# Ten transposed K blocks instead of six kept between two passes over a KV cache

## The chip, the cores and the metric

The kernel runs on one core of one Trainium2 chip. The metric is the device time of one execution in microseconds (us). A core has a matrix engine (TensorE, PE in the profile; PEld is its weight load), a vector engine (VectorE, DVE), a scalar engine (ScalarE, ACT), GpSimd (POOL), a queue engine that here only issues loads (SyncE, SP), and 16 DMA engines between the off-chip memory (HBM) and the on-chip memory of 128 partitions (SBUF). PE writes its results to PSUM, from which DVE or ACT copy them ("evacuation").

## The reference

Two kinds of layers alternate twice on one token `x` of 1024 elements: attention over a cache, then an MLP with squared ReLU. Both attention layers use the same weights and the same cache, and so do both MLPs. The reference returns the output and the gradients of everything for a given `grad_out`.

```python
x = x + A(layernorm(x));  x = x + B(layernorm(x))
x = x + A(layernorm(x));  x = x + B(layernorm(x))

# A: 32 query heads on 4 key/value heads, 65536 cached positions, head size 128
q = (x @ wq)                      # 1024 -> 32 x 128
scores = q . k_cache * 128**-0.5  # 8 query heads share one key/value head
o = softmax(scores) . v_cache
return o @ wo
# B: 3584 hidden
h = x @ w1 + b1;  r = max(h, 0);  return (r * r) @ w2 + b2
```

K and V are 64 MiB each in bfloat16 (4 groups of 16 MiB); their gradients, which are written, have the same size.

## The kernel before, in words

**Four passes over the cache.** Pass 1 is the forward of the first attention layer (L1), then comes the first MLP (L2), pass 2 is the forward of the second attention layer (L3), then the second MLP and its backward (L4); passes 3 and 4 are the backward of the two attention layers. Each pass reads all of K and V. The "first boundary" is the MLP L2 between pass 1 and pass 2. Pass 1 takes the groups in order 0, 1, 2, 3 (`ORD1`), pass 2 in order 3, 2, 1, 0 (`ORD2`), so that the group that ends pass 1 begins pass 2.

**Items and blocks.** A group has 512 chunks of 128 positions. An *item* is 8 chunks (64 items a group, `IPG`), a *block* is 4 items, 1 MiB of K or V (16 blocks a group). `attn_fwd` runs a software pipeline over 256 items (`pipeline`): at step i it does `kT` of item i, `kS` of item i-2 and `v8` of item i-78 (`TLEAD` = 2, `LAGV` = 78).
- `kT` transposes 8 K chunks on PE into a PSUM tile `ps_tr` (L656) and evacuates them to one of five blocks of `small`, on DVE or ACT (`evac`, L152 and L155, whichever has the smaller planned load).
- `kS` multiplies them with the queries (L675); every 64 chunks ACT copies the scores to a score buffer (L680) and DVE takes maxima (L681). Behind a group's last item, `stats` forms the maximum and ACT the exponentials (L704) into `eT`.
- `v8` multiplies 8 V chunks with the exponentials (L718).
Since V of a group needs the group's maximum, V runs 78 items behind K.

**Side work.** `bg` holds functions that run at a given step. `q_rest` loads 8 rows of `wq` (768 KB each) and multiplies them with the token, for the queries of the three later groups: row k at step 20 + 4k. `out_group` loads the two slabs of `wo` of a finished group and multiplies (products on L399, in `mv_slab`).

**The memory areas.** SBUF holds 14 areas of 8 KB per partition (`area[0]` to `area[13]`, two to a `pair`), the exponentials `eT1` and `eT3` of both layers, and `small`. `pair[10]` (areas 10, 11) and `pair[12]` (areas 12, 13) are the score buffers `S0` and `S1`, used by the groups in turn. Areas 0 to 9 form the ring (`Ring`): each load takes the area that was taken longest ago (`slot`), or, for a wide load of two blocks (2 MiB), a pair whose halves are both in the ring (`wide`). During pass 1 the space of `eT3`, which the second layer fills only later, lends four areas (`e3_halves`); they leave the ring 9 steps before the last group.

**The order of the loads.** All loads of this part are issued by SyncE in one queue, in the order in which they are written; a load waits in it until the readers of its area's former content are done, and what is written behind it waits too. A load has no other place in time: it goes as early as its area and the queue let it. The framework's scheduler may move instructions on an engine; "built order" means the order in which they stand in the finished program.

**What is kept.** In pass 1 the transposed blocks of group 3 that `keep` names stay where `kT` evacuates them. In pass 2 `kT` neither loads nor transposes the blocks in `have`; `kS` reads them where they lie. `kept1` has six: one in the space of each of the four groups of `eT3`, two in `S0`, which the last group of pass 1 does not use (it writes to `S1`).

**Around the boundary.** Behind pass 1 stand `out_group` of group 3, 8 slabs of `B_w1` (L399), 7 slabs of `B_w2`, which are multiplied (L399) and also row-multiplied with `grad_out` for a later gradient (`RowDots`: L421, L422, L457, L468 to L476), then two slabs of `wq` for the first group of pass 2 (`q_first`), all through the ring.

Of the kernel before, what the change touches and what calls it, by code (L numbers as in the profile page):

```python
# [18 lines left out]
def kernel(  # L19
# [27 lines left out]
    G = A_k_cache.shape[1]  # L47
# [20 lines left out]
    IPG = C // 8  # L68
# [48 lines left out]
    def ps_bg(shape, dtype=F32):  # L117
        return ps_small("bg", shape, dtype)
# [50 lines left out]
    area, pair, wides = [], {}, []  # L169
# [5 lines left out]
    e3_halves = [e3_all[:, i * SLOT:(i + 1) * SLOT] for i in range(4)]  # L175
# [4 lines left out]
    def e_area(k, g):  # L180
        return e_tiles[k][g][:, 0:SLOT]

    def part(ap, i, n):
        return ap[:, i * n:(i + 1) * n]
# [11 lines left out]
    class Ring:  # L196
# [35 lines left out]
        def wide(self):  # L232

            best = None
            for w, lo, hi in wides:
                h = [s for a in (lo, hi) for s in self.slots if s["ap"] is a and not s["held"]]
                if len(h) == 2:
                    t = max(s["used"] for s in h)
                    if best is None or t < best[0]:
                        best = (t, w, h)  # L240
            for s in best[2]:
                s["used"] = self.clock
                self.clock += 1
            return best[1], [s["ap"] for s in best[2]]

        def hold(self):

            s = self.last
            s["held"] = True

            def give():
                s["held"] = False
            return give

    ring = Ring()
# [14 lines left out]
    def slab(src, a, n):  # L270
        v = ring.slot()[:, 0:a * n].rearrange("p (a n) -> p a n", n=n)
        nc.sync.dma_start(out=v, in_=src)
        return v
# [109 lines left out]
    def w_rows(W, r0, nk, c0, ncol):  # L383

        return W[r0:r0 + nk * P, c0:c0 + ncol].rearrange("(k p) n -> p k n", p=P)

    def slabs(W, r0, KC, c0, ncol):

        per = max(1, min(KC, SLOT // ncol))
        for k0 in range(0, KC, per):  # L390
            kn = min(per, KC - k0)
            v = slab(w_rows(W, r0 + k0 * P, kn, c0, ncol), kn, ncol)
            for kk in range(kn):
                yield k0 + kk, v[:, kk, :]

    def mv_slab(out, view, kc, KC, ncol, xcol):
        nb_ = ncol // P
        for nb in range(nb_):
            nc.tensor.matmul(out[:, nb:nb + 1], lhsT=view[:, nb * P:(nb + 1) * P], rhs=xcol,  # L399
                             start=(kc == 0 and nb == 0), stop=(kc == KC - 1 and nb == nb_ - 1), skip_group_check=True)  # L400
# [186 lines left out]
    def at(bg, i, fn):  # L587
        bg.setdefault(i, []).append(fn)

    def q_first(L, g):  # L590

        pq = ps_bg([P, R])
        for kc, view in slabs(A_wq, 0, DC, g * GD, GD):
            mv_slab(pq, view, kc, DC, GD, L["nb"][:, kc:kc + 1])
        set_q(L, pq, 0, [g])

    def set_q(L, pq, at_, gs):
        for i, g in enumerate(gs):
            nc.vector.tensor_copy(out=L["qT"][:, g * R:(g + 1) * R], in_=pq[:, (at_ + i) * R:(at_ + i + 1) * R])
            nc.vector.tensor_copy(out=L["qpad"][:, g, :, :], in_=L["qT"][:, g * R:(g + 1) * R].unsqueeze(1).to_broadcast([P, 8, R]))  # L600

    def q_rest(L, gs, bg, i0, step):
        gs = sorted(gs)
        c0, ncol = gs[0] * GD, len(gs) * GD
        assert gs == list(range(gs[0], gs[0] + len(gs)))
        box = {}

        def one(kc):
            if kc == 0:
                box["p"] = ps_bg([P, len(gs) * R])  # L610
            v = slab(w_rows(A_wq, kc * P, 1, c0, ncol), 1, ncol)
            mv_slab(box["p"], v[:, 0, :], kc, DC, ncol, L["nb"][:, kc:kc + 1])
            if kc == DC - 1:
                set_q(L, box["p"], 0, gs)
        for kc in range(DC):
            at(bg, i0 + kc * step, lambda kc=kc: one(kc))
# [8 lines left out]
    def new_layer(x, lname):  # L625
        n, nb, rstd = ln_fwd(x, lname)
        L = dict(n=n, nb=nb, rstd=rstd)
        for key, w, dt in (("qT", HQ, F32), ("oT", HQ, F32), ("oTb", HQ, BF), ("rZ", HQ, F32), ("xo", DC, F32)):
            L[key] = vec.tile([P, w], dt, name=lname + "_" + key)
        L["qpad"] = vec.tile([P, G, 8, R], BF, name=lname + "_qpad")  # L630
        nc.vector.tensor_copy(out=L["xo"][:], in_=x[:])
        return L

    def attn_fwd(L, order, eT, s_areas, more=None, keep=(), have=()):

        kit = items_of(order)
        n = len(kit)
        bg = {}
        if more is not None:
            more(bg, n - 1 + TLEAD)  # L640
        q_rest(L, order[1:], bg, 20, 4)
        for j, g in enumerate(order[:-1]):
            at(bg, LAGV + IPG * (j + 1) + 4, lambda g=g: out_group(L, g))
        kstream, vstream = Stream(Kv, True), Stream(Vv, True)
        state = {}

        def kT(idx):
            g, c8 = kit[idx]
            b, j = divmod(c8, J)
            if g == order[0] and b < len(have):  # L650
                state[("kt", idx)] = blocks(have[b], j // 8)
                return
            kb8 = kstream.items(g, c8)
            pt = ps_tr()
            for i in range(8):
                nc.tensor.transpose(pt[:, i, :], kb8[:, i, :], ident_b[:, :])  # L656
            kt = blocks(keep[b], j // 8) if g == order[-1] and b < len(keep) else KT.next()
            evac(kt[:, :, :], pt[:, :, :])
            state[("kt", idx)] = kt
# [475 lines left out]
    eT1, eT3 = Exps(1), Exps(3)  # L1135
    U, X1 = area[0:5], area[5:10]
    S0, S1 = pair[10], pair[12]
# [3 lines left out]
    L1 = new_layer(x0, "L1")  # L1141
    ORD1, ORD2, ORD3, ORD4 = [0, 1, 2, 3], [3, 2, 1, 0], [0, 1, 2, 3], [3, 2, 1, 0]
# [2 lines left out]
    b2c = col_from_dram(B_b2, D, "b2c")  # L1145
    gx = col_from_dram(grad_out.rearrange("a b d -> (a b d)"), D, "gx")

    kept1 = [e_area(3, g) for g in range(G)] + [area[10], area[11]]
    ring.add(*e3_halves)

    def ahead_of_last(bg, ik):
        at(bg, IPG * (G - 1) - 9, lambda: ring.remove(*e3_halves))
    attn_fwd(L1, ORD1, eT1, [S0, S1], more=ahead_of_last, keep=kept1)


    out_group(L1, ORD1[-1])
# [11 lines left out]
    dg4 = rd4.result()  # L1168
    L3 = new_layer(L2["xo"], "L3")
    q_first(L3, ORD2[0])  # L1170


    VKEEP = 4
# [2 lines left out]
    def fetch_w1(a=None):  # L1176
        v = (a if a is not None else ring.slot())
        w1_slots.append(v)
        nc.sync.dma_start(out=v[:, 0:F], in_=B_w1[len(w1s) * P:(len(w1s) + 1) * P, :])
        w1s.append(v[:, 0:F])  # L1180
# [10 lines left out]
    def wo_block(k, out=None, scalar=True):  # L1191

        v = kept[k][1] if out is None else out
        transpose(kept[k][1], v, scalar)
        woT[k] = [part(v, i, P) for i in range(DC)]

    def ahead_of_end(bg, ik):
        e = ik + 1 - TLEAD + LAGV
        at(bg, e - 28, fetch_wo)
        for k, i in ((0, 4), (1, 7)):  # L1200
            at(bg, e - 12 + 4 * k, lambda k=k, i=i: wo_block(k, part(small, i, 1024), k == 0))
        at(bg, e - 6, lambda: (fetch_w1(area[12]), fetch_w1(area[13])))
    v_areas = attn_fwd(L3, ORD2, eT3, [S1, S0], more=ahead_of_end, have=kept1)
    v_kept = [v_areas[(ORD2[-1], b)] for b in range(NB - VKEEP, NB)]


# [24 lines left out]
    bg = {}  # L1231
# [125 lines left out]
    bg = {}  # L1357
# [67 lines left out]
```

## Time and profile before

| | us |
|---|---|
| median of 3 runs | 2000.78 (1998.74 to 2001.92) |
| profiled execution, its time | 2006.47 |
| profiled execution, its span | 2004.7 |
| pass 1 | 0 to about 368 |
| products of `B_w1` and `B_w2`, layer norm | about 372 to 421 |
| first score product of pass 2 | 423.1 |
| pass 2 until its last V product | 423 to 770 |
| bytes moved by DMA | 798 MB, mean 398 GB/s |
| PE / DVE / ACT busy | 80% / 55% / 51% of the span |

Times inside an execution are in microseconds from the start of the span. A row of groups of instructions gives line, engine, operation, output and input tiles, shape and count. "PEclk" is the granted share of TensorE's full clock. "DMA share" is the mean busy share of the 16 DMA engines (overlap can bring it slightly above 1). On SyncE's timeline a row stands for one or more loads issued, and its duration is that of issuing, not of the transfer.

### The profile page before, as it was taken

The page shows a single profiled execution, that of the slowest core. Times are in us where ns is not written, and L with a number is a line of the kernel's source. Part 1 is how long each engine was busy: PE and PEld are TensorE (multiplying, and loading weights), DVE is VectorE, ACT ScalarE, POOL GpSimd, SP SyncE. Part 2 cuts the span into 40 slices and gives each one's busy share as a digit, 9 for nine tenths or more (in the row PEclk, how much of TensorE's full clock was granted, in tenths as well). Part 3 has the DMA queues.
Part 4 walks back from the last instruction along what each step waited for, and adds up shares of the span by engine and source line. Part 5 has one row for each costly group of instructions (what it writes and reads, how often), then busy time and mean ns, then how long its engine had stood idle before and what let it go on. Part 6 is the DMA issues. An engine that isn't in the chain of part 4 may idle for free.

```text
span 2004.7 us, 66048 instructions
## 1 busy us (share of the span) xinstructions
PE 1599.8 (80%) x30052; PEld 1320.6 (66%) x30052; DVE 1108.3 (55%) x1826; ACT 1032.3 (51%) x1290; POOL 203.3 (10%) x362
## 2 busy tenths in 40 slices
PE   7888776678888867887878876877888878778896
PEld 6888776578787756876777774555555545545463
DVE  4544431255444313745454446876677767787675
ACT  3543432125433313445454436876677667767775
POOL 0000000000000000000000001222122222212221
PEclk9999997679999976998989987999889988899898
DMA  9999999999999996999999996999999999999997
GB/s 395 426 424 421 419 422 413 395 368 376 424 421 419 423 414 272 399 418 409 411 413 393 403 372 261 389 425 424 389 413 407 423 423 383 422 358 422 423 422 293
DMA packets 117316, 798.08 MB, mean 398 GB/s; under 512 B 11548, under 2 KB 11562, under 8 KB 55082
## 3 DMA queue, kind: packets, MB, share of 16 engines
q1 hardware_dynamic: 80986, 608.22, 74.0%
q0 software_dynamic: 29136, 173.04, 20.9%
q10 hardware_dynamic: 6912, 12.59, 1.7%
q8 instruction: 235, 3.85, 0.7%
q14 instruction: 47, 0.39, 0.0%
HBM read 628.11 MB, written 165.69 MB: 396 GB/s over the span
## 4 chain that ended last, share of the span: by engine, by line
PE 39%; DMA 30%; DVE 12%; ACT 11%; issue 7%; POOL 0%; SPq 0%; DVEq 0%; ACTq 0%; POOLq 0%
DMA pair<-in_A_v_cache_dram 13%; DMA out_dram<-pair 8%; PE ps_tr L656 7%; DMA pair<-in_A_k_cache_dram 5%; PE ps_sc L675 4%; ACT small L152 4%; PE ps_tr L909 4%; PE ps_acc L718 3%; PE ps_gg L1071 3%; PE ps_tr L1004 3%; ACT pair L152 3%; DVE pair L155 3%; DVE small L155 2%; PE ps_sc L930 2%; PE ps_gg L1122 2%
## 5 line engine op out<-in xcount | busy, mean ns | idle before, releaser
L155 DVE COPY small<-ps_tr 128x1024 bf16<-128x1024 bf16 x655 | 445.2, 688 | 356.1 <-PE ps_tr L656 197.8
L152 ACT COPY small<-ps_tr 128x1024 bf16<-128x1024 bf16 x385 | 386.6, 1014 | 410.1 <-PE ps_tr L656 234.1
L152 ACT CAST pair<-ps_gg 128x1024 bf16<-128x1024 f32 (+2 forms) x331 | 320.2, 983 | 143.2 <-PE ps_gg L1071 81.8
L155 DVE CAST pair<-ps_gg 128x1024 bf16<-128x1024 f32 x245 | 289.2, 1181 | 115.6 <-PE ps_gg L1071 89.0
L656 PE MATMUL ps_tr<-ident_b,pair 128*128 128x128 bf16 x3456 | 263.4, 225 | 34.6 <-DMA pair<-in_A_k_cache_dram 25.4
L1071 PE MATMUL ps_gg<-pair,small 64*128 64x512 bf16 x1024 | 202.9, 405 | 53.8 <-ACT pair L152 21.5
L656 PEld LDWEIGHTS <-pair 128*128 128x128 bf16 x3456 | 209.5, 101 | 39.7 <-DMA pair<-in_A_k_cache_dram 27.8
L675 PE MATMUL ps_sc<-L_qpad,small 128*128 128x64 bf16 (+7 forms) x3712 | 187.5, 194 | 27.1 <-ACT small L152 13.9
L718 PE MATMUL ps_acc<-eT,pair 128*128 128x64 bf16 x3840 | 167.1, 205 | 44.9 <-DMA pair<-in_A_v_cache_dram 39.6
L718 PEld LDWEIGHTS <-pair 128*128 128x128 bf16 x3840 | 151.9, 104 | 48.5 <-DMA pair<-in_A_v_cache_dram 42.4
L675 PEld LDWEIGHTS <-small 128*128 128x128 bf16 x3712 | 151.5, 99 | 38.5 <-ACT small L152 20.1
L1004 PE MATMUL ps_tr<-ident_b,pair 128*128 128x128 bf16 x1792 | 163.3, 229 | 14.1 <-DMA pair<-in_A_v_cache_dram 12.0
L422 ACT ACTIVATE pair<-pair 128x1024 bf16<-128x1024 bf16 (+1 forms) x125 | 142.1, 1137 | 45.6 <-DVE pair L421 43.6
L909 PE MATMUL ps_tr<-ident_b,pair 128*128 128x128 bf16 x2048 | 153.5, 227 | 10.4 <-DMA pair<-in_A_v_cache_dram 5.4
L1004 PEld LDWEIGHTS <-pair 128*128 128x128 bf16 x1792 | 115.6, 102 | 60.5 <-issue 41.5
L909 PEld LDWEIGHTS <-pair 128*128 128x128 bf16 x2048 | 126.7, 102 | 30.8 <-issue 20.7
L1071 PEld LDWEIGHTS <-small 64*128 64x128 bf16 x1024 | 60.5, 94 | 111.3 <-issue 83.8
L930 PE MATMUL ps_sc<-B_dOpad,small 128*128 128x64 bf16 (+7 forms) x2048 | 103.0, 194 | 21.5 <-DVE small L155 13.9
L1024 PE MATMUL ps_sc<-DOB,small 128*128 128x64 bf16 (+3 forms) x2048 | 111.7, 194 | 0.1
L1024 PEld LDWEIGHTS <-small 128*128 128x128 bf16 x2048 | 86.6, 99 | 36.8 <-issue 32.2
L930 PEld LDWEIGHTS <-small 128*128 128x128 bf16 x2048 | 81.2, 99 | 32.8 <-DVE small L155 17.5
L681 DVE TENSOR_REDUCE pm_all<-pair 128x8 f32<-128x512 f32 x64 | 44.0, 688 | 106.1 <-ACT pair L680 106.1
(262 smaller groups left out, 1966.2 us busy)
## 6 DMA issues: line engine op xcount, KB each, us to landing
pair<-in_A_v_cache_dram SPq DMA_DIRECT2D x70, 2048.0 KB, 19.9
pair<-in_A_k_cache_dram SPq DMA_DIRECT2D x65, 2048.0 KB, 19.5
out_dram<-pair POOLq DMA_DIRECT2D x128, 1024.0 KB, 16.2
pair<-in_A_k_cache_dram SPq DMA_DIRECT2D x97, 1024.0 KB, 12.4
pair<-in_A_v_cache_dram SPq DMA_DIRECT2D x96, 1024.0 KB, 12.8
pair<-in_A_wo_dram SPq DMA_DIRECT2D x24, 1024.0 KB, 20.3
out_dram<-eT POOLq DMA_DIRECT2D x44, 512.0 KB, 15.6
pair<-in_B_w_dram SPq DMA_DIRECT2D x24, 896.0 KB, 16.7
```

Source lines behind the costliest of these rows:

```text
L152: nc.scalar.copy(out=out, in_=in_)
L155: nc.vector.tensor_copy(out=out, in_=in_)
L422: nc.scalar.activation(out=view, in_=view, func=ACTF.Copy, accum_out=ycol)
L656: nc.tensor.transpose(pt[:, i, :], kb8[:, i, :], ident_b[:, :])
L675: nc.tensor.matmul(ps_s[:, slot:slot + w, :].rearrange("p a b -> p (a b)"), lhsT=kt[:, i, :], rhs=L["qpad"][:, g, 0:w, :].rearrange("p a b ...
L681: nc.vector.tensor_reduce(out=pm_all[:, :, c0 // UB], in_=S_sb[:, :, c0:c0 + un], axis=AX.X, op=ALU.max)
L718: nc.tensor.matmul(ps_o[:, :, :].rearrange("p a b -> p (a b)"), lhsT=vb8[:, i, :], rhs=eT[g][:, :, c:c + 8], start=(c == 0), stop=(c == C ...
L909: nc.tensor.transpose(pt[:, i, :], vb8[:, i, :], ident_b[:, :])
L930: nc.tensor.matmul(ps_dp[:, slot:slot + w, :].rearrange("p a b -> p (a b)"), lhsT=vt[:, i, :], rhs=dOpad[:, g, 0:w, :].rearrange("p a b -> ...
L1004: nc.tensor.transpose(pt[:, i, :], vb8[:, i, :], ident_b[:, :])
L1024: nc.tensor.matmul(ps_dp[:, slot:slot + w, :].rearrange("p a b -> p (a b)"), lhsT=vt[:, i, :], rhs=DOB[:, g, 0:w, :].rearrange("p a b -> p ...
L1071: nc.tensor.matmul(pg[:, t2 * 512:(t2 + 1) * 512], lhsT=xt[64 * t2:64 * t2 + 64, blk0 + half, :], rhs=GG[64 * t2:64 * t2 + 64, :, :, :].re ...
```

## The change

- `kept1` becomes ten areas: the four `e3_halves`, areas 10 and 11, and two pairs of the ring. These two pairs are taken out of the ring while the last group of pass 1 runs (`take_pair`, 14 and 22 steps into it), always the pair that was used longest ago. From then on the ring has six areas.
- From 6 steps into the last group to 8 steps behind its K items, `narrow` makes K and V come in loads of one block instead of two.
- `S1` (areas 12, 13) joins the ring behind the last group's exponentials, through the rest of pass 1, the MLP and `q_first`, and then leaves it.
- In pass 2 each kept area outside `S0` joins the ring one step after its last item's scores; the four `e3_halves` leave it at step 52, before the exponentials are written there.
- In pass 2 the rows of `q_rest` come at step 2 + 3k instead of 20 + 4k.

```diff
+        def take_pair(self):
+            halves = self.wide()[1]
+            self.remove(*halves)
+            return halves
...
-    def attn_fwd(L, order, eT, s_areas, more=None, keep=(), have=()):
+    def attn_fwd(L, order, eT, s_areas, more=None, keep=(), have=(), q_at=(20, 4), narrow=None):
...
-        q_rest(L, order[1:], bg, 20, 4)
+        q_rest(L, order[1:], bg, *q_at)
...
+        def width(wide):
+            kstream.wide = vstream.wide = wide
+        for i, wide in zip(narrow or (), (False, True)):
+            at(bg, i, lambda wide=wide: width(wide))
...
-    kept1 = [e_area(3, g) for g in range(G)] + [area[10], area[11]]
+    kept1 = e3_halves + [area[10], area[11]]
     ring.add(*e3_halves)
+    last = IPG * (G - 1)
     def ahead_of_last(bg, ik):
-        at(bg, IPG * (G - 1) - 9, lambda: ring.remove(*e3_halves))
-    attn_fwd(L1, ORD1, eT1, [S0, S1], more=ahead_of_last, keep=kept1)
+        at(bg, last - 9, lambda: ring.remove(*e3_halves))
+        for i in (last + 14, last + 22):
+            at(bg, i, lambda: kept1.extend(ring.take_pair()))
+        at(bg, last + IPG + 7, lambda: ring.add(area[12], area[13]))
+    attn_fwd(L1, ORD1, eT1, [S0, S1], more=ahead_of_last, keep=kept1, narrow=(last + 6, last + IPG + 8))
...
     q_first(L3, ORD2[0])
+    ring.remove(area[12], area[13])
...
     def ahead_of_end(bg, ik):
+        for b, a in enumerate(kept1):
+            if not any(a is x for x in (area[10], area[11])):
+                at(bg, 4 * b + 5, lambda a=a: ring.add(a))
+        at(bg, IPG - 12, lambda: ring.remove(*e3_halves))
...
-    v_areas = attn_fwd(L3, ORD2, eT3, [S1, S0], more=ahead_of_end, have=kept1)
+    v_areas = attn_fwd(L3, ORD2, eT3, [S1, S0], more=ahead_of_end, have=kept1, q_at=(2, 3))
```

## The prediction

> **What bounds the kernel now.** I read the page first (engines, DMA row, chain), then stretches of time, then SyncE's queue around the first boundary, then PE there. The page's DMA row stands at 9 in almost all of its 40 slices, and among the chain's costliest rows are loads. The stretches (columns: span in us; busy us and instructions of PE, PEld, DVE, ACT, POOL; granted clock; DMA share; GB/s) say where this is strict:
>
> ```profile
> PE 39%; DMA 30%; DVE 12%; ACT 11%; issue 7%; POOL 0%; SPq 0%; DVEq 0%; ACTq 0%; POOLq 0%
> ...
> 0.00:320.00 320.00, 263.13 (x6028) 250.23 (x6029) 141.40 (x261) 133.02 (x180) 1.03 (x10) 0.98 1.00 417
> 320.00:380.00 60.00, 35.44 (x786) 33.73 (x782) 2.90 (x17) 6.55 (x17) 0.00 (x0) 0.67 1.00 407
> 380.00:424.00 44.00, 28.78 (x630) 27.46 (x631) 21.21 (x57) 17.30 (x27) 0.00 (x0) 0.50 1.02 392
> 424.00:462.00 38.00, 32.95 (x815) 31.72 (x813) 20.05 (x36) 7.02 (x10) 0.61 (x4) 0.93 0.80 306
> 462.00:766.00 304.00, 238.32 (x5477) 228.19 (x5474) 113.86 (x190) 113.30 (x165) 0.00 (x0) 0.92 1.01 420
> 1060.00:1080.00 20.00, 17.68 (x424) 16.31 (x421) 8.14 (x11) 8.06 (x9) 0.00 (x0) 1.00 1.02 418
> ```
>
> Pass 1 (to about 368) and pass 2 from 462 on are DMA-bound: share 1.00 and 1.01, PE busy for 0.8 of the time. There a load that is left out shortens the pass by its own transfer, whatever PE does. The exception is 424 to 462, the start of pass 2: share 0.80, so 7.6 us of DMA time are lost. SyncE's queue shows why (start, us of issuing, what):
>
> ```profile
> 402.75 0.48 SPq L295 DMA_DIRECT2D pair<-in_A_k_cache_dram  x1
> 403.33 1.78 SPq L272 DMA_DIRECT2D pair<-in_A_wq_dram  x2
> 414.72 0.33 SPq L295 DMA_DIRECT2D pair<-in_A_k_cache_dram  x1
> 417.37 4.55 SPq L272 DMA_DIRECT2D pair<-in_A_wq_dram  x2
> 429.61 0.33 SPq L295 DMA_DIRECT2D pair<-in_A_k_cache_dram  x1
> ...
> 446.34 12.08 SPq L295 DMA_DIRECT2D pair<-in_A_k_cache_dram  x3
> 465.57 0.33 SPq L295 DMA_DIRECT2D pair<-in_A_v_cache_dram  x1
> ...
> SPq L295 <- PE ps_bg L399: 11.2, 2, 7.6
> SPq L295 <- PE ps_tr L656: 10.9, 1, 10.9
> SPq L272 <- PE ps_tr L656: 10.7, 3, 4.2
> ```
>
> The loads wait for PE to leave a ring area (the last three rows: who waited, total us, times, longest). The three K loads from 446.34 are issued at 446.34, 457.62 and 458.04 in the records; from the second on DMA is full again. PE at the same place:
>
> ```profile
> 423.11 5.17 PE L675 MATMUL ps_sc<-L_qpad,eT 128*128 128x64 bf16 x128 [0.49 <-DVE L_qpad L600]
> 428.83 0.74 PE L399 MATMUL ps_bg<-L_nb,pair 128*128 128x1 bf16 x24
> 429.44 1.28 PE L675 MATMUL ps_sc<-L_qpad,pair 128*128 128x64 bf16 x40
> ```
>
> A kept item (8 score matmuls) costs 0.31 us up to 429.4 and 0.23 after; one row of `wq` (24 products) 0.6. A K item that must be transposed costs 0.86 to 1.1 us here, evacuation waits included (40 of them end at 477.3, from 430.7; the last 23 took 19.9 us).
>
> **The change, part by part.** The sum is made on the profiled execution (span 2004.7, time 2006.47, 5.7 over the median of 2000.78) and moved to the median unchanged.
>
> 1. *Four K blocks less to load.* In the built program K reads fall from 250 to 246 MiB. 4.19 MB at the 420 GB/s of 462:766 are 10.0 us. With them go 16 items' transposes (0.45 us of PE each) and their evacuations, which lie beside the DMA and pay nothing directly.
>
> 2. *The start of pass 2* decides whether the 10.0 us arrive. All eight `wq` rows now stand ahead of the first K load in SyncE's queue, and in the built order of PE their products come after 5, 12, 19, 26, 33, 39, 40 and 40 kept items. Slots: rows 0 to 4 go where parts of `B_w2` lay (the last two leave at 414.7 and 417.4), row 5 where the first `wq` slab lay (421.6), row 6 where row 0 lay, row 7 into a consumed kept block. They land by about 430, none is late. The first K pair (blocks 10 and 11) takes the area of rows 2 and 3. PE gets through row 3 at: 16 items and two rows by 429.4, then 9.4 items x 0.23 + 1.2 = 432.8. A load on an empty queue shows its first packet 1.0 us after issue (429.61 to 430.6, 457.62 to 458.6), and 2.1 MB take 5.0: landing 438.8. PE is through its 40 items at 438.4, so it waits for almost nothing. Blocks 12 to 15 and group 2's first pair follow without a gap (areas free by 431, 437.1 and 437.9): 443.8, 448.8, 453.8. Before, group 2's first pair was issued at 457.62 and landed at 458.6 + 5.0 = 463.6. From this load on both kernels send the same loads, so the pass is **9.8 us** ahead. DMA idles more than before up to 434 and less after it. For the queue to stay full PE must leave the pair of block 15 by 468: 438.4 + 24 items x 0.86 to 1.0 = 459 to 462. Bounds: if blocks 10 and 11 wait for the 40th item (438.4), 4.2; if their area is free with row 2 (430.6), 12.0.
>
> 3. *Narrow loads at the end of pass 1.* In the built order 30 loads of 1 MiB stand in place of 15 of 2 MiB. In the packet records a 16 KB packet takes 619 ns and an 8 KB one 317 to 321 (pass 3), so 1 MiB over 16 engines takes 2.48 or 2.54 to 2.57 us: 30 x 0.06 to 0.09 = 1.8 to 2.7, taken as **+2.3**. The bytes are the same, so no gain is possible: low end 0. High end: pass 3 from 1040 to 1120, with the same two narrow streams, five or six areas left and more side work, moves 395 GB/s on average (395, 418, 393, 373); 31.5 MB at 395 instead of 420 is +4.7. I take the packets, since the side work of pass 3 is absent here.
>
> 4. *Six areas in place of ten for items 214 to 263.* A 1 MiB area is wanted again 8 to 9 items before its data is needed, which at 0.5 MiB an item leaves four loads, about 10 us, in the queue; PE needs 3.9 us for the 4 items that one K and one V block feed (32 transposes 1.8, 32 score matmuls 0.9, 32 products 1.1 at full clock), DMA 5.1. Cost 0; the cover is that queue. The products of the second group's `A_wo` (64, 1.9 us) stand whole behind both of its slabs, with four loads in flight, 10 us: 0.
>
> 5. *The score buffer in the ring.* The second V pair of the last group now waits for ACT's exponentials, and every later load queues behind it on SyncE. Before, the last K pair landed at 308.6, PE was through it at 314, the exponentials ran from 319.25 to 324.8. In the narrow order (one block, 4 items, 2.7 us) they end 2.7 + 5.3 + 5.6 = 13.6 us after the last K block. Queued behind that block are four V blocks, one V pair and two `A_wo` slabs, 8.4 MB or 20 us. Hidden, with 6 us to spare; beyond that it would cost one for one.
>
> 6. *Eight areas through the MLP.* Each part of `B_w2` waits for the slab of `B_w1` eight loads earlier, which itself is paced by landing (the products of the last two slabs start at 385.19 and 387.4). Queue never empty: 0. The stretch 390 to 417 is computation and not touched. Dropping areas 12 and 13 from the ring, and adding the kept areas to it, issue nothing.
>
> Sum: -9.8 + 2.3 = **-7.5 us**: 1993.3 on the median. Behind pass 2 the built order is the same but for about a hundred PE instructions and three exchanges of loads, so the lead is carried to the end.
>
> **Rivals.**
>
> *Narrow loads starve the DMA (slower).* If every second narrow load meets an empty queue and pays its 1.0 us lead-in, 15 us go: 2000.8 - 9.8 + 2.3 + 15 = 2008.3. It decides from 0.25 us per narrow load (7.5/30). For it: only six areas, and two streams locked to each other. Against: 1060:1080, share 1.02 at 418 GB/s with as few areas. Chance 0.12. The Trainium skill ("DMA: Bandwidth & Descriptors", Measured) gives 341 GB/s for a lone DMA of 1 MB and 425 for 16 MB, and asks for large batches; by its figure the 31.5 MB would cost an estimated 17 us more and the change would lose some 7. The 418 GB/s of that stretch disagree, because other loads are in flight there.
>
> *The start of pass 2 gives it back (no change).* The first K load is held until the 40th kept item and pass 3's 395 GB/s hold in the tail: -4.2 + 4.7, about 2001.3; with only one of the two, 1996 to 1999. For it: loads before 462 wait for PE already (11.2 us under `ps_bg`), and DMA will idle some 10 us between 410 and 434. Against: PE runs kept items at 0.23 to 0.31 us, so areas come free sooner than now. Chance 0.16.
>
> *That fewer loads are not made* is excluded by the built program's 246 MiB.
>
> **How the numbers follow.** What a measurement of this kernel can tell from no change is 0.2%, 4 us (the three runs shown spread 0.16%). The forecast, a gain over 4 us: 0.72; within 4 us: 0.16; slower: 0.12. The range takes parts 2 and 3 at their ends: -12.0 + 0 gives 1988.8, -4.2 + 4.7 gives 2001.3; it leaves out the starved tail.
>
> **What would show it.** Part 1: K bytes less by 4.19 MB, pass 2 still at 420 GB/s. Part 2: the first K load of pass 2 near 433 (plus the tail's shift), the full queue from about 434 on instead of 458. Part 3: last V landing of pass 1 2 to 3 us later, share 1.00 throughout. Part 5: no gap of the DMA 15 to 20 us after the last K block of pass 1. Wrong it would be if the stretch 250 to 320 showed a share clearly under 1, or if PE in pass 2 waited for K loads beyond the first.

## The result, and the profile after

The changed kernel is faster: 1995.0 us median (1993.3 to 1998.2) against 2001.6 for the kernel before on the same chip, a ratio of 0.997 with a 95% interval of 0.996 to 0.998. That is 6.6 us less, where 7.5 were predicted. Measured again on another chip it gave 1993.3 against 1999.9, 0.9967 (0.9955 to 0.9979).

The stretches of the changed kernel (columns as before: span in us; busy us and instructions of PE, PEld, DVE, ACT, POOL; granted clock; DMA share; GB/s):

```profile
0.00:320.00 320.00, 265.79 (x6024) 250.25 (x6025) 141.02 (x261) 134.36 (x184) 1.04 (x10) 0.97 1.00 414
320.00:380.00 60.00, 35.38 (x762) 33.38 (x758) 2.86 (x17) 5.07 (x12) 0.00 (x0) 0.64 1.00 410
380.00:424.00 44.00, 28.63 (x639) 27.29 (x640) 20.83 (x55) 17.35 (x27) 0.00 (x0) 0.50 0.94 355
424.00:462.00 38.00, 34.15 (x871) 33.66 (x869) 19.50 (x36) 6.13 (x9) 0.61 (x4) 0.85 0.87 348
462.00:766.00 304.00, 237.39 (x5446) 227.75 (x5445) 109.67 (x191) 108.26 (x159) 0.00 (x0) 0.92 1.01 419
```

The DMA-bound stretches are DMA-bound still: 1.00 in pass 1, 1.01 at 419 GB/s from 462 on. At the boundary the idle time of the DMA has moved: less of it after 424 (share 0.87, was 0.80), more before (0.94 in 380 to 424, was 1.02). SyncE's queue there:

```profile
396.43 31.39 SPq L278 DMA_DIRECT2D pair<-in_A_wq_dram  x9
427.87 0.42 SPq L278 DMA_DIRECT2D eT<-in_A_wq_dram  x1
435.02 0.33 SPq L301 DMA_DIRECT2D pair<-in_A_k_cache_dram  x1
435.40 0.42 SPq L301 DMA_DIRECT2D eT<-in_A_k_cache_dram  x1
439.55 4.30 SPq L301 DMA_DIRECT2D pair<-in_A_k_cache_dram  x3
451.07 0.33 SPq L301 DMA_DIRECT2D pair<-in_A_v_cache_dram  x1
```

All ten loads of `wq` stand ahead of the first K load, which is issued at 435.0. The three from 439.55 are issued at 439.55, 443.05 and 443.43 in the records; the one at 443.05 is group 2's first pair, 14.6 us earlier than before (457.62). In the records of landings that pair is complete at 458.4, and at 459.0 in a second execution (e12), instead of 466.9: 8.5 and 7.9 us ahead. PE there:

```profile
438.78 0.74 PE L405 MATMUL ps_bg<-L_nb,pair 128*128 128x1 bf16 x24
439.38 0.27 PE L686 MATMUL ps_sc<-L_qpad,pair 128*128 128x40 bf16 x5
439.51 0.54 PE L405 MATMUL ps_bg<-L_nb,pair 128*128 128x1 bf16 x16
442.67 0.35 PE L405 MATMUL ps_bg<-L_nb,pair 128*128 128x1 bf16 x8 [2.62 <-issue]
442.88 0.78 PE L405 MATMUL ps_bg<-L_nb,eT 128*128 128x1 bf16 x24
443.52 2.72 PE L667 MATMUL ps_tr<-ident_b,pair 128*128 128x128 bf16 x24
```

The 40 kept items are through at 439.5 (predicted 438.4), but the transposes begin at 443.5: a row of `wq` stops in its middle for 2.6 us ("issue": nothing that the profile shows was waited for).

What that was worth shows in the last division of each pass. The line that forms the outputs of a group, first of the kernel before, then of the changed one (last column: first and last start):

```profile
L722 DVE TENSOR_TENSOR L_oT<-ps_acc,L_rZ x8: 166/167/168, 157.6 to 769.7; 128x8 f32<-128x8 f32 x8
```

```profile
L733 DVE TENSOR_TENSOR L_oT<-ps_acc,L_rZ x8: 166/167/168, 157.6 to 762.5; 128x8 f32<-128x8 f32 x8
```

The end of pass 2 is 7.2 us earlier (7.8 in the second execution). The end of pass 1 (fourth of the eight) is at 369.1 instead of 368.1.

**A ledger of bytes.** The packet records give, for each kernel, the time at which it has moved as many bytes as the kernel before had at a time T. In pass 1 that is its lag. In pass 2 the MiB that it no longer loads are taken off first, so the figure is its lead (minus) in the same work. "Start" is what the boundary adds: the figure at T = 600, less that at 410, plus 2.5 us for each MiB left out. Each row is one profiled execution against one of the kernel before. In "at 600" and "start" the two rows of the changed kernel differ by 1.5 us, so differences under 2 us tell nothing there. The lag repeats better: at 320 it is 2.4 to 2.8 in the eight rows whose pass 1 is that of the changed kernel up to there (changed, again, e4, e5, e7, e8, e9, e10).

| kernel | kept | MiB less | lag at 320 | lag at 410 | at 600 | start | median, us | ratio (95%) |
|---|---|---|---|---|---|---|---|---|
| e1, narrow loads only | 6 | 0 | 1.2 | 1.3 | -1.4 | -2.7 | +2.3 | 1.002 (1.0009 to 1.0031) |
| e2 | 8 | 2 | 1.4 | 1.1 | -5.2 | -1.3 | -4.4 | 0.9977 (0.9967 to 0.9986) |
| changed kernel | 10 | 4 | 2.6 | 1.9 | -7.5 | +0.6 | -6.6 | 0.997 (0.996 to 0.998) |
| changed kernel, again | 10 | 4 | 2.6 | 1.9 | -6.0 | +2.1 | -6.5 | 0.9967 (0.9955 to 0.9979) |
| e3, wide loads | 10 | 4 | 7.2 | 5.8 | -6.0 | -1.8 | -6.3 | 0.9973 (0.9961 to 0.9986) |
| e4, rows late | 10 | 4 | 2.4 | 1.5 | -7.8 | +0.7 | -6.4 | 0.9972 (0.996 to 0.9983) |
| e5, no score buffer | 10 | 4 | 2.6 | 2.9 | -6.2 | +0.9 | -3.5 | 0.9976 (0.9964 to 0.9988) |
| e7, first pairs early | 10 | 4 | 2.6 | 1.8 | -5.1 | +3.1 | -5.5 | 0.9974 (0.9964 to 0.9985) |
| e10, e4 and e7 | 10 | 4 | 2.7 | 1.9 | -5.8 | +2.3 | -4.5 | 0.9981 (0.9969 to 0.9993) |
| e8, kept blocks loaded too | 10 | 0 | 2.8 | 1.9 | +3.0 | +1.1 | +4.2 | 1.0023 (1.0013 to 1.0032) |
| e9, kept blocks transposed too | 10 | 4 | 2.7 | 1.9 | -4.7 | +3.4 | -3.6 | 0.9984 (0.9975 to 0.9994) |
| e6 | 12 | 6 | 7.3 | 8.5 | -2.8 | +3.7 | -2.9 | 0.9985 (0.9977 to 0.9994) |
| e11, e6 with rows late | 12 | 6 | 5.7 | 6.9 | -6.3 | +1.8 | -3.7 | 0.998 (0.9966 to 0.9994) |

"Median" is the difference from the kernel before on the same chip; the ratio is a second estimate, and the two differ by up to 1.7 us (e1: +2.3 and +4.0). The column at 600 agrees with it within 3 us everywhere but in e1, whose profiled execution was the fastest of its twelve, 4.8 us under their median. So what this change does is done by T = 600.

### The profile page after: what moved, and what is told of

It reads as the page before. It is cut to its first block, busy times and chain, and to the rows that moved or that the text cites. A ratio compares the mean times of both kernels' runs of the same rounds, so it can differ in the third digit from the quotient of the medians.

```text
span 1994.9 us, 65729 instructions
## 1 busy us (share of the span) xinstructions
PE 1590.6 (80%) x29868; PEld 1316.1 (66%) x29924; DVE 1101.0 (55%) x1816; ACT 1026.5 (51%) x1284; POOL 204.4 (10%) x362
## 3 DMA queue, kind: packets, MB, share of 16 engines
HBM read 623.92 MB, written 165.69 MB: 396 GB/s over the span
## 4 chain that ended last, share of the span: by engine, by line
PE 38%; DMA 34%; DVE 10%; ACT 10%; issue 7%; another core or an unknown queue 0%; POOL 0%; SPq 0%; ACTq 0%; POOLq 0%; DVEq 0%
DMA pair<-in_A_v_cache_dram 15%; DMA pair<-in_A_k_cache_dram 8%; DMA out_dram<-pair 7%; PE ps_tr L667 6%; PE ps_sc L686 4%; PE ps_acc L729 4%; PE ps_gg L1082 4%; PE ps_tr L920 3%; PE ps_tr L1015 3%; ACT small L152 3%; ACT pair L152 3%; DVE pair L155 3%; DMA pair<-in_A_wo_dram 2%; DVE small L155 2%; PE ps_sc L941 2%
## 5 line engine op out<-in xcount | busy, mean ns | idle before, releaser
L155 DVE COPY small<-ps_tr 128x1024 bf16<-128x1024 bf16 x637 | 432.2, 688 | 338.1 <-PE ps_tr L667 172.8
L152 ACT COPY small<-ps_tr 128x1024 bf16<-128x1024 bf16 x371 | 372.8, 1015 | 387.6 <-PE ps_tr L667 206.8
L667 PE MATMUL ps_tr<-ident_b,pair 128*128 128x128 bf16 x3264 | 246.8, 225 | 29.2 <-DMA pair<-in_A_k_cache_dram 16.4
L667 PEld LDWEIGHTS <-pair 128*128 128x128 bf16 x3264 | 197.4, 101 | 34.8 <-DMA pair<-in_A_k_cache_dram 19.0
L686 PE MATMUL ps_sc<-L_qpad,small 128*128 128x64 bf16 (+7 forms) x3456 | 173.9, 193 | 24.0 <-issue 10.7
L729 PEld LDWEIGHTS <-pair 128*128 128x128 bf16 x3840 | 154.0, 104 | 48.3 <-DMA pair<-in_A_v_cache_dram 42.9
L1015 PE MATMUL ps_tr<-ident_b,pair 128*128 128x128 bf16 x1792 | 163.4, 229 | 14.8 <-DMA pair<-in_A_v_cache_dram 11.6
L920 PE MATMUL ps_tr<-ident_b,pair 128*128 128x128 bf16 x2048 | 155.6, 228 | 13.6 <-DMA pair<-in_A_v_cache_dram 9.8
L686 PEld LDWEIGHTS <-small 128*128 128x128 bf16 x3456 | 140.4, 99 | 34.6 <-ACT small L152 16.1
L1015 PEld LDWEIGHTS <-pair 128*128 128x128 bf16 x1792 | 115.7, 102 | 61.3 <-issue 42.8
L920 PEld LDWEIGHTS <-pair 128*128 128x128 bf16 x2048 | 128.6, 103 | 35.7 <-DMA pair<-in_A_v_cache_dram 17.8
L1035 PEld LDWEIGHTS <-small 128*128 128x128 bf16 x2048 | 87.0, 100 | 36.9 <-issue 32.0
L941 PEld LDWEIGHTS <-small 128*128 128x128 bf16 x2048 | 80.1, 99 | 26.1 <-ACT small L152 14.1
```

Source lines behind the costliest of these rows:

```text
L152: nc.scalar.copy(out=out, in_=in_)
L155: nc.vector.tensor_copy(out=out, in_=in_)
L686: nc.tensor.matmul(ps_s[:, slot:slot + w, :].rearrange("p a b -> p (a b)"), lhsT=kt[:, i, :], rhs=L["qpad"][:, g, 0:w, :].rearrange("p a b ...
L729: nc.tensor.matmul(ps_o[:, :, :].rearrange("p a b -> p (a b)"), lhsT=vb8[:, i, :], rhs=eT[g][:, :, c:c + 8], start=(c == 0), stop=(c == C ...
L920: nc.tensor.transpose(pt[:, i, :], vb8[:, i, :], ident_b[:, :])
L941: nc.tensor.matmul(ps_dp[:, slot:slot + w, :].rearrange("p a b -> p (a b)"), lhsT=vt[:, i, :], rhs=dOpad[:, g, 0:w, :].rearrange("p a b -> ...
```

## The experiments

**Are the bytes the gain? (e8)** The changed kernel, with the four added kept blocks loaded in pass 2 all the same, and read by nobody. Their transposes stay left out. By the code the two loads stand at steps 124 and 132 (100 + 4 x 6 and 100 + 4 x 8), not 100 and 108 as the expectation has it; both places lie in the stretch that the DMA bounds.

```diff
+        def again(b):
+            kstream.fetch(order[0], b)
+            for i in range(2):
+                kstream.ahead.pop((order[0], b + i))
+        if have:
+            for b in (6, 8):
+                at(bg, 100 + 4 * b, lambda b=b: again(b))
```

> After, and the four added kept blocks are loaded from HBM in pass 2 all the same, at its steps 100 and 108, and never read (no transposes): their bytes are back, TensorE's saved work is not. Theory (the gain is the bytes: 4.19 MB at 419 GB/s in a stage whose DMA share is 1.01): +10 us against after, +3 against before (range +1 to +4); end of pass 2 near 772. Rival (the gain is that pass 2 starts its products earlier, on TensorE): stays at -6 us.

It lost 4.2 us against before, ratio 1.0023 (1.0013 to 1.0032): 10.8 us more than the changed kernel's first measurement, for 4.19 MB (9.0 to 10.5 by the column at 600). The end of pass 2 went back too:

```profile
L741 DVE TENSOR_TENSOR L_oT<-ps_acc,L_rZ x8: 165/167/168, 157.6 to 770.6; 128x8 f32<-128x8 f32 x8
```

The boundary is as in the changed kernel (lag at 410 1.9, start +1.1); only the bytes differ. Shown: the gain is the bytes, at about the predicted price of 10.0 us, and everything else that the change brings, the saved transposes included, is a net cost of about 3 us at T = 600, 4.2 by the medians.

**And TensorE's saved work? (e9)** The reverse: the loads stay left out, and the 16 items are transposed and evacuated again, from the kept blocks, into an area that nobody reads (added where `kT` skips a kept block).

```diff
+                if b >= 6:
+                    again = state[("kt", idx)]
+                    pt = ps_tr()
+                    for i in range(8):
+                        nc.tensor.transpose(pt[:, i, :], again[:, i, :], ident_b[:, :])
+                    evac(KT.next()[:, :, :], pt[:, :, :])
```

> After, and for the four added kept blocks TensorE makes eight transposes per item again (16 items, of the kept block itself) and their eviction is made again, into an area that nobody reads; no load is added. So the saved work of TensorE is back and the saved bytes are not. Theory (bytes): within 1 us of after, -6 us against before. Rival (TensorE sets the pace until the V loads run, 440 to 485): 16 x about 0.65 us, up to 10 us of the gain lost, -2 to +3 us against before.

It kept 3.6 us of the gain, 0.9984 (0.9975 to 0.9994), which meets neither expectation: some 3 us are lost, of the 10 that the rival had. The stretches 410 to 440 and 440 to 490 of the changed kernel, then of this one:

```profile
410.00:440.00 30.00, 24.92 (x684) 24.09 (x685) 10.97 (x33) 8.57 (x17) 0.00 (x0) 0.69 0.71 258
440.00:490.00 50.00, 43.14 (x942) 41.64 (x940) 32.62 (x59) 18.50 (x32) 0.61 (x4) 0.93 1.00 418
```

```profile
410.00:440.00 30.00, 25.97 (x642) 24.47 (x643) 17.10 (x43) 6.93 (x12) 0.00 (x0) 0.85 0.73 264
440.00:490.00 50.00, 41.93 (x991) 40.73 (x988) 29.13 (x54) 24.40 (x38) 0.61 (x4) 0.97 0.99 393
```

The DMA stays busy to 0.99 behind 440, but moves 393 GB/s where the changed kernel moves 418. The work did not come back in the place from which it was saved: on PE's timeline the added transposes run from 416.8 to 428.3, ahead of the kept items' scores and in part in the idle time of the layer norm, and the first score product of pass 2 starts at 428.5 instead of 424.7. Up to T = 470 this costs nothing (lead 7.9, as the changed kernel with 7.8 and 7.1); then the lead falls to 5.0 at 490. In between, a V load that the changed kernel issues at 463.1 goes at 469.6, because PE leaves its area later. So TensorE's saved work is worth 1 to 3 us of the 10 by the ledger, at the edge of what it can tell; what the same work would cost in its old place is not shown.

**What do narrow loads cost? (e1)** The kernel before, with the narrow loads alone (the parameter `narrow` and `width` as in the change, and this call).

```diff
...
-    attn_fwd(L1, ORD1, eT1, [S0, S1], more=ahead_of_last, keep=kept1)
+    attn_fwd(L1, ORD1, eT1, [S0, S1], more=ahead_of_last, keep=kept1, narrow=(IPG * (G - 1) + 6, IPG * G + 8))
```

> The kernel before with nothing but the narrow loads in the last group of pass 1 (six kept blocks, ten ring areas). Theory (an 8 KB packet is a little slower per byte, nothing else): +1.8 to +2.7 us against before, DMA share still 1.00 in 240 to 320 us. Rival 1 (the lock-step of two narrow streams stalls by itself): +5 us or more, share under 1. Rival 2 (what the changed kernel loses in its tail comes from having six areas, not from narrow loads): 0.

+2.3 us by the medians, ratio 1.002 (1.0009 to 1.0031): as its theory had it, but somewhere between +1.8 and +6.2 by the interval. The stretch 240 to 320 of the kernel before, of e1 and of the changed kernel:

```profile
240.00:320.00 80.00, 65.74 (x1567) 62.76 (x1565) 32.09 (x53) 28.18 (x34) 0.00 (x0) 0.98 1.00 417
```

```profile
240.00:320.00 80.00, 68.42 (x1575) 63.66 (x1572) 31.79 (x53) 29.21 (x36) 0.00 (x0) 0.97 1.01 413
```

```profile
240.00:320.00 80.00, 68.04 (x1569) 63.23 (x1567) 31.66 (x53) 29.48 (x38) 0.00 (x0) 0.98 1.00 405
```

In all three the DMA is never short of work. It moves 4 GB/s less with narrow loads and 12 less with narrow loads on six areas: 80 x 12/419 = 2.3 us, of which 0.8 are the narrow loads' alone. Most of the rest is lost while the ring shrinks and not on the six areas as such: of the 1.4 us by which the changed kernel lags behind e1 at 320, 1.0 arises between 240 and 260, when the two pairs are taken out. From 260 to 320 it moves 413 to 417 GB/s, e1 417 to 419. The mean packet of the load queue in this stretch was 619 ns for 16 KB before; for 8 KB it was 316 in e1 and 318 in the changed kernel, 2 to 3% dearer by the byte.

**Does the small ring need them? (e3)** The changed kernel with loads of two blocks kept.

```diff
-    attn_fwd(L1, ORD1, eT1, [S0, S1], more=ahead_of_last, keep=kept1, narrow=(last + 6, last + IPG + 8))
+    attn_fwd(L1, ORD1, eT1, [S0, S1], more=ahead_of_last, keep=kept1)
```

> The changed kernel with loads of 2 MiB kept to the end of pass 1, so that six areas are three pairs. Theory (six areas suffice only because the loads are narrow): a K pair then waits for the transposes of the items just ahead of it, so each of some five K pairs shows its lead-in and transfer (1 + 5 us) less what V loads cover: pass 1 ends 15 to 25 us later than in the changed kernel, whole kernel +8 to +18 us against before. Rival (six areas suffice for either size): -9 us, since the 2.3 us of the packets are saved.

-6.3 us, 0.9973 (0.9961 to 0.9986): as the changed kernel. The expected loss did not come.

```profile
240.00:320.00 80.00, 63.30 (x1518) 60.77 (x1514) 30.58 (x48) 26.85 (x30) 0.00 (x0) 0.98 0.96 385
```

```profile
PE ps_acc L729 <- DMA pair<-in_A_v_cache_dram: 22.5, 11, 3.9
PE ps_tr L667 <- DMA pair<-in_A_k_cache_dram: 12.1, 8, 2.7
```

Wide loads do leave the DMA short of work in this stretch, in which the ring shrinks from ten areas to six, but by 4% only (0.96 x 80 leaves 3.2 us idle), and PE waits 12.1 us for K loads from 200 to 372, against 7.1 in the changed kernel. Lag at 410: 5.8 us, 3.9 more than the changed kernel. At 600 it is even with the second execution of the changed kernel and 1.5 us behind the first. The DMA has slack at the start of pass 2 (share 0.71 from 410 to 440 in the changed kernel), and most of the lag went into it: "start" is -1.8 here. So in this run the delay in the tail of pass 1 is not paid one for one, and in this kernel the narrow loads bring nothing that can be measured.

**How many blocks to keep? (e2, e6)** One pair of areas taken out of the ring in place of two (e2, eight kept), and three (e6, twelve kept, four areas left):

```diff
-        for i in (last + 14, last + 22):
+        for i in (last + 14,):
```

```diff
-        for i in (last + 14, last + 22):
+        for i in (last + 14, last + 22, last + 30):
```

> After, but only the first pair of areas is taken out of the ring: eight K blocks are kept in place of ten, and the tail of pass 1 runs on a ring two areas larger. Theory (the time goes with the bytes: each kept block saves 1.05 MB, 2.5 us at 415 GB/s, of which narrow loads take 2.3 us once): two blocks less are -5.0, +2.3 for the narrow loads, about -2.7 us against the kernel before (range -4 to -1), that is some 4 us slower than after; end of pass 2 near 766. Rival (what counts is that K loads may start before the last of pass 1 is consumed, whatever their number): as after, -6 to -7 us.

> After, with a third pair of areas taken out of the ring eight steps later: twelve K blocks kept in place of ten, four areas left for the last products of V in pass 1. Theory (bytes): two blocks more are -5.0 against after, less what the tail of pass 1 loses on four areas, 0 to 8 us; about -8 us against before (range -14 to 0). Rival (TensorE already sets the pace between 440 and 485, as the run with earlier first pairs suggests): fewer bytes change nothing, the time stays at -6 to -7 us or gets worse by the tail alone.

Eight: -4.4 us, 0.9977 (0.9967 to 0.9986), better than the bytes had it (-2.7, range -4 to -1), and not told apart from ten by the intervals. Twelve: -2.9 us, 0.9985 (0.9977 to 0.9994): 3.7 us worse than ten, where the bytes alone would give 5 us more. Stretches of the run with twelve:

```profile
240.00:320.00 80.00, 67.62 (x1562) 62.79 (x1559) 31.83 (x53) 28.04 (x34) 0.00 (x0) 0.98 0.97 384
320.00:340.00 20.00, 7.46 (x171) 6.80 (x167) 0.91 (x6) 6.25 (x16) 0.00 (x0) 0.68 0.92 351
410.00:440.00 30.00, 23.74 (x598) 23.24 (x599) 12.52 (x37) 9.88 (x17) 0.46 (x3) 0.62 0.74 260
440.00:490.00 50.00, 42.25 (x1029) 40.85 (x1026) 29.20 (x55) 16.46 (x30) 0.15 (x1) 0.97 0.94 384
```

```profile
434.49 2.53 SPq L278 DMA_DIRECT2D pair<-in_A_wq_dram  x2
443.73 9.11 SPq L301 DMA_DIRECT2D pair<-in_A_k_cache_dram  x4
```

Two things are late. In the tail four areas leave the DMA idle (0.97 and 0.92): a lag of 8.5 us at 410 in place of 1.9. And the first K load of pass 2 is issued at 443.7 in place of 435.0, behind the rows of `wq`, which have to pass through the same few areas; 4.1 us of these 8.7 are there already when pass 2 starts (first score product at 428.8, not 424.7). DMA is idle 7.8 us to 440 and 3.0 more to 490 (shares 0.74 and 0.94), 10.8 in all, against 8.7 in the changed kernel. An area that keeps a block is one that the queue cannot fill ahead of time.

**Which of the two? (e11)** Twelve kept, with the rows of `wq` back at their old steps.

```diff
-    v_areas = attn_fwd(L3, ORD2, eT3, [S1, S0], more=ahead_of_end, have=kept1, q_at=(2, 3))
+    v_areas = attn_fwd(L3, ORD2, eT3, [S1, S0], more=ahead_of_end, have=kept1)
```

> Twelve kept, with the rows' steps back at (20, 4). Theory (in the run with twelve kept the first K load of pass 2 was issued at 443.7, behind the rows' weights, which go through the same areas; in after it was 435.0): the first K load comes at 430 to 436, the DMA idle of 410 to 490 falls from 11.5 to about 8 us, and the time by 3 to 5 us, to -6 to -8 against before. Rival (the loss lies in the tail of pass 1, 3.3 us at its end on four areas): stays near -3.

-3.7 us, 0.998 (0.9966 to 0.9994): by the medians the expected 3 to 5 us did not come, and the rival (the tail) fits. But the edit did not do what the theory needs: the first K load came at 439.6, not at 430 to 436, and the idle time of the DMA from 410 to 490 stayed at 10.5 us. The lag at 410 was 6.9 us. That is 5 us more than with ten kept, as much as the two further blocks save, and the start adds about what it adds with ten (+1.8); so in this execution the tail takes back the gain of the two blocks (-6.3 at 600, as the changed kernel). Why the start took up a part of such a lag in e3 and none of it here is not shown.

**Do the rows' steps matter with ten? (e4)** The same edit in the changed kernel.

> The changed kernel with the wq rows of pass 2 at their former steps (20 + 4k). In the built order the first K pair then stands behind row 4 and goes to consumed kept blocks; the second waits for row 1's product, which PE reaches only behind some 25 items. Theory (the rows' steps matter only by which area the first K loads get): within 2 us of the changed kernel, 5 to 9 us faster than before. Rival (moving the rows is what makes the ten blocks pay): the gain falls to 2 us or less against before.

-6.4 us, 0.9972 (0.996 to 0.9983), as the changed kernel. Within the noise they do not.

**Can the idle DMA of 410 to 440 be used? (e7, e10)** Both make the consumed blocks of the `e3_halves` the next areas to be taken, for the first two K pairs of pass 2; e10 has the edit of e4 as well.

```diff
+    def old_first(*aps):
+        ring.add(*aps)
+        for n, s in enumerate(ring.slots[-len(aps):]):
+            s["used"] = n - len(aps)
...
-            if not any(a is x for x in (area[10], area[11])):
+            if not any(a is x for x in (*e3_halves, area[10], area[11])):
                 at(bg, 4 * b + 5, lambda a=a: ring.add(a))
+        at(bg, 30, lambda: old_first(*e3_halves))
```

> The changed kernel, but the first two K pairs of pass 2 go to the four consumed kept blocks in the space of eT3, so that the first K load can go near 428.5 us instead of 435.0. Theory A (DMA idle between 410 and 436 is paid in full, as my sum has it): up to 6 us faster than the changed kernel, 12 us faster than before. Theory B (behind the kept items PE sets the pace until V starts, since from the 48th item on each load waits for PE to leave a pair): at most 1 us faster than the changed kernel, 6 to 8 us faster than before; the load queue fills earlier and then waits for PE between 460 and 490 us.

> After with both edits that alone gave nothing: the first two K pairs of pass 2 go into the consumed halves, and the rows' steps are back at (20, 4). Theory (the hole at 485 to 490, DMA share 0.30, which the run with early first pairs showed, is TensorE being late with the areas, since the rows' products lie in the same stretch; 9 to 10 us of DMA idle between 410 and 490 are what is left to gain): without the rows there the hole closes, 2 to 4 us better than after, -9 to -11 against before. Rival (the four transposed groups alone keep TensorE busy until 485, or the areas come free no earlier): -5.5 to -7, as each alone.

e7: -5.5 us, 0.9974 (0.9964 to 0.9985). e10: -4.5 us, 0.9981 (0.9969 to 0.9993). Neither beats the changed kernel. The stretches of e7:

```profile
410.00:440.00 30.00, 21.28 (x560) 20.40 (x560) 10.68 (x31) 8.10 (x14) 0.00 (x0) 0.70 0.81 302
440.00:490.00 50.00, 45.97 (x1021) 44.83 (x1021) 31.80 (x58) 18.21 (x31) 0.60 (x4) 0.86 0.92 373
```

The first K load is issued at 430.2 instead of 435.0, and the share before 440 rises from 0.71 to 0.81; behind it, it falls from 1.00 to 0.92, because the next areas are not free yet (SyncE waits 15.0 us for PE's transposes on one load). 3.0 us won, 4.0 lost. In e10 that hole closed (share 1.01 from 440 to 490), as its theory had it, but one opened ahead of it (0.62 from 410 to 440). SyncE's queue in e10 shows why:

```profile
398.89 11.48 SPq L278 DMA_DIRECT2D pair<-in_A_wq_dram  x4
426.00 2.04 SPq L278 DMA_DIRECT2D eT<-in_A_wq_dram  x2
```

Two rows of `wq` took the consumed halves that were meant for a K pair. They waited there until pass 2 had read the kept blocks, from 410.4 to 426.0, and everything behind them waited too: the DMA share from 415 to 425 is 0.15. So e10 did not make the load order that its theory speaks of, and that order stays untested. What stays is that a load here needs an area that PE has left, and these edits only changed which load got it first.

**Does the score buffer in the ring matter? (e5)** The changed kernel without it.

```diff
-        at(bg, last + IPG + 7, lambda: ring.add(area[12], area[13]))
...
-    ring.remove(area[12], area[13])
```

> After, but the free score buffer never joins the ring: after pass 1 the weights of the MLP and of the first row of pass 2 stream through six areas in place of eight. Theory (the stage's loads are queued well ahead either way): as after, -6.6 us against before, within 1.5 us. Rival (six areas starve the MLP's weights, whose stage runs at a DMA share of 1.00 to 1.04): first K block of pass 2 two to six us later than 435, gain down to -1 to -5 us.

-3.5 us by the medians, -4.8 by the ratio: 0.9976 (0.9964 to 0.9988). That lies between the two expectations, and its interval covers the changed kernel's value. In its trace the MLP was not starved (share 1.02 and 1.05 in 372 to 390 and 390 to 410, as in the changed kernel), the first K load of pass 2 came at 432.5, not later than 435, and the end of pass 2 (762.7) is that of the changed kernel. Only the tail of pass 1 is a little worse (share 0.96 from 320 to 340, was 0.99; lag at 410 2.9, was 1.9). So the rival's mechanism is absent, but the time leaves 0 to 3 us open.

**The changed kernel again (e12).** To learn whether such differences of 2 to 3 us mean anything:

> The changed kernel itself once more, since the runs without the score buffer, with early first pairs and with twelve kept blocks lie 2 to 3 us above its first measurement, inside the intervals. If those differences are real, it comes out at -6 to -7 us against before again (ratio 0.9965 to 0.9970); if they are the spread between measurements, nearer to -4 or -5 (0.9975 to 0.9980).

-6.5 us, 0.9967 (0.9955 to 0.9979), so the measurement repeats. No other run is faster by its median. The intervals of e2, e3, e4, e5, e7, e10 and e11 reach its 0.997, those of e1, e6, e8 and e9 do not.

## Why the prediction was right, point by point

- **Sum:** -7.5 predicted; -6.6 and -6.5 measured, and -7.2 and -7.8 at the end of pass 2 in the profiled executions. The medians agree with that lead within 1.3 us, so behind pass 2 nothing systematic was added, as said. Split by e8, the medians give -10.8 for the bytes and +4.2 for all the rest, where -10.0 and +2.5 were forecast. Each is right within the noise of about 2 us; that the two deviations cancel in the sum is in part luck.
- **Part 1, the bytes (10.0 us):** right. HBM reads fell from 628.11 to 623.92 MB, pass 2 stayed at 419 GB/s, and loading the four blocks all the same gave 10.8 us back (e8). That the saved transposes pay nothing directly is not settled: with them back in another place 3 us are lost (e9).
- **Part 2, the start (-9.8):** right in size, a little off in its steps. The first K load was forecast at 433 plus the tail's shift of about 2 and came at 435.0; the idle time of the DMA between 410 and 440 is 8.7 us (0.29 x 30), "some 10" was said. The share is 1.00 from 437 on (438 in e12), where 434 plus that shift was forecast, and stays at 1.00 to 490. By the ledger 7.9 to 9.4 us of the 10.0 come through the boundary ("start" +0.6 and +2.1). The load on which the term was worked out, group 2's first pair, lands 8.5 and 7.9 us ahead with the tail's delay in it; 9.8 - 2.3 = 7.5 was forecast. Both worked landings were too early (453.8, measured 458.4; before 463.6, measured 466.9), which nearly cancels in the difference. What it had not seen is PE's pause of 2.6 us in a row of `wq` (the kernel before has one of 1.8 us there); it was covered, since the queue was full by then.
- **Part 3, narrow loads (+2.3):** the sum right, the division not. The lag is 2.6 us at 320 and 1.9 at 410, but with ten areas narrow loads alone lag 1.2 (e1), though e1's median is 2.3 worse. The rest (1.4 at 320) comes with the smaller ring, which **part 4** had at 0: 1.0 of it while the two pairs are taken out (240 to 260), so for the six areas as such the 0 is nearly right. The forecast of a share of 1.00 throughout held; what falls is the rate (405 instead of 417). The end of pass 1 is 1.0 us later, not 2 to 3.
- **Parts 5 and 6, the score buffer and the MLP (0):** no gap of the DMA 15 to 20 us after the last K block (share 0.95 in 325 to 330, 0.25 us). In part 6 the stretch 380 to 424 has lost share (0.94), but because the loads that used to fill its end are gone, not because the MLP waits (share 1.02 to 1.05 up to 410).
- **The signs of being wrong:** neither came. The share of 250 to 320 is 1.01, and from 430 to 490 PE waits for no K load; its 5.9 us of such waits from 490 to 760 (14.3 in e12, 12.3 before) belong to the stretch that the DMA bounds.
- **The starved tail (rival, slower):** did not happen; it needed 0.25 us for each narrow load, and all thirty cost about 2 us together by the ledger. The estimate of 17 us beside it, from the Trainium skill ("DMA: Bandwidth & Descriptors", Measured, where a DMA of 1 MB has 341 GB/s, issued from GpSimd and not from SyncE as here), is not borne out: 1 MiB loads with others behind them moved at 405 to 413 GB/s. The direction of that table in the Trainium skill holds, larger transfers are cheaper by the byte, but here by 2 to 3%.
- **The start gives it back (rival, no change):** did not happen with ten. With twelve a part of it did: the first K load came 8.7 us later than with ten and the tail lagged by 8.5 us, and only 2.9 us of 15 remained.

The prediction took a delay in the tail as paid one for one. In e3 the start of pass 2 took up a part of it (lag 5.8 at 410, "start" -1.8), in e6 and e11 it did not; with a tail lag of only 2 us this made no difference to the sum.

## What to carry to other kernels

Where the DMA is the bound, a block that stays on the chip is worth its own transfer time, and the way to check is to load it all the same: the time must come back. But every area that keeps data is one that the queue cannot fill ahead, so the number that pays has an end: -4.4 us with eight kept, -6.6 with ten (these two are not told apart by their intervals), -2.9 with twelve, where the lag at 410 had grown from 1.9 to 8.5 us. A ledger of bytes moved against time, kernel against kernel, shows where the lead is won and lost when the medians differ by a few us only.

## What the runs showed of the hardware that was not expected

- **PE pauses beside packets of instructions.** In the stretch where PE runs short products (one column at about 25 ns each, scores at about 30), it stopped for 2.62 us at 440.0 in the changed kernel, and for 1.76 us before 437.6 and 2.45 us before 443.9 in e9, and the profile names no cause. In the packet records a 16 KB packet of the queue named "instruction" starts at 440.32 in the first, and at 435.21 and 441.41 in the second, each taking 0.94 to 0.95 us; in this stretch such packets come every 3 to 7 us. This is no accident of one trace: in the fourteen traces there are 124 stops of PE of over 1.2 us without a named cause, and every one of them ends 2.2 to 2.6 us after the start of such a packet. Most packets have no such stop (234 packets and 11 stops in the changed kernel). That PE waited for its own instructions fits, but no run changed what would test it.
- **More work, higher clock.** With the added transposes of e9 the granted clock of 410 to 440 was 0.85, with the changed kernel's work 0.69 (0.61 to 0.74 in the other twelve traces). The transposes begin at 416.8, and from 420 to 430 the clock is 1.00 in e9 and 0.57 in the changed kernel. Part of the added work may have been paid by that; it is not separated here.
- **Four per cent for a smaller ring.** With loads of 2 MiB and a ring that shrinks from five pairs to three (e3), the DMA share of 240 to 320 was 0.96 instead of 1.00, far from the starvation that was expected.
